# Small instructions of a top-k attention and mixture-of-depths kernel move from VectorE to GpSimd and ScalarE

## The chip, the cores and the metric

The kernel runs on one core of a Trainium2 chip. The metric is device time in microseconds of one execution; less is better. Five engines of the core work from queues of their own, each in the order of its program: TensorE (PE in profiles, PEld for its weight loads), VectorE (DVE), ScalarE (ACT), GpSimd (POOL) and SyncE (SP), which issues most of the DMAs.

## The reference

Two blocks follow each other. The first is attention over 8 batches, 8 heads, 576 tokens and a head size of 64, in which each query keeps its 32 highest scores:

```python
scores = scale * np.matmul(q, k.transpose(0, 1, 3, 2))
kth = np.partition(scores, -top_k, axis=-1)[..., -top_k:-top_k + 1]
scores = np.where(scores >= kth, scores, -1000000000.0)
attn = np.exp(scores - np.max(scores, axis=-1, keepdims=True))
attn = attn / (np.sum(attn, axis=-1, keepdims=True) + 1e-09)
x = np.matmul(attn, v)          # then (B, S, H*D) = (8, 576, 512)
```

The second is a mixture of depths: the 128 tokens of a batch with the highest gate score pass through a two-layer network, weighted by the sigmoid of their gate, and the other tokens stay:

```python
scores = np.einsum('bsd,d->bs', x, w_gate)
top_idx = np.argpartition(-scores[b], capacity)[:capacity]
ye = np.maximum(x[b, top_idx] @ w1, 0.0) @ w2
g = 1.0 / (1.0 + np.exp(-scores[b, top_idx]))
out[b, top_idx] = x[b, top_idx] + g[:, None] * ye
```

## The kernel before, in words

**Units and steps.** A batch's 576 tokens make five tiles: four of 128 tokens (`J` = 4) and one of 64. A unit is a tile and two heads (four heads in the short tile), so a batch has 18 units and the whole 144. The main loop is a software pipeline over the units. Step `n` does at once: the products of queries and keys of unit n+1 on TensorE and their copy to `sc` by ScalarE; `bound_of(n)` on VectorE, which finds a lower bound of the 32nd highest score by 14 MAX8 over parts of the row and a few more over the candidates; `sign(n-1)` on ScalarE, which compares each score with the bound (`sides`); `weigh_signs(n-1)` on GpSimd, which multiplies scores and signs to `y` and fills eight more columns; `kth_of(n-2)` on VectorE, two long MAX8 (`next`) that give the 32nd score; `mask_of(n-3)`, in which ScalarE marks what is below it for one head and GpSimd for the other (`less`); the transposes, exponentials (`pT`, `last`) and products with the values for unit n-4, and the copy of the values to `xs`.

**Order.** Every engine's instructions are kept in program order. Work that should stand late in a step is put on lists as a function and called at fixed places of the step: `late` (flushed on ScalarE between the mask and the copy of the scores), `vector_late` (between the two heads' first MAX8), `pool_late` (after that, ahead of `y`), `kept` (after the copy of the values) and `after_kth` (after `kth_of`, on VectorE). There is no planner; the steps at which the pieces of the second block run are written by hand in `mix_at` and `mix_at_of`.

**A finished tile.** In the step in which the last unit of a tile is done, `keep_sums` (line 710) has ScalarE copy the sums of the exponentials out of `xs` into `sums`. In the next step `normalise` runs from `vector_late`: a reciprocal `rden` on VectorE, then a product on GpSimd. A step later `gates` multiplies the tile with the gate weights (`prod`, `gate`). After the fifth tile the batch is stored, and `mixture` (line 761) starts, a generator whose pieces run in the following steps.

**The mixture.** It splits the gates into three bf16 parts (`split`), sends the gates through DRAM to have all 576 on every partition (`gate_row`), and then, tile by tile, counts on VectorE how many gates are higher (`choose`, line 800), which is the token's rank. A comparison of the rank with the numbers 0 to 127 gives a 0/1 matrix `pick`; for the first tile VectorE makes it in the same place, for the others GpSimd does (`choose_slot`). Five matmuls of `pick` with the parts put each slot's token number and gate, in three parts each, into PSUM. ScalarE copies them to `found`, and `add_up` (line 846) on VectorE adds the parts, forms the row number `row_i` and clips the gate; ScalarE takes the exponential, and `squash` adds one and inverts. GpSimd fetches the rows with an indirect DMA, TensorE multiplies, and GpSimd adds the result to the rows in DRAM with another.

**Masks beside scatters.** At the six `scatter_steps` the second half of the mask is not GpSimd's but VectorE's (`mask_of(n - 3, (act, None) ...)`, line 1207), through `vector_late`.

**Checks.** At the end VectorE reduces what was kept of the bounds (`bounded`, copied by ScalarE in `keep_least`), `least`, `seen` and `sums` to one number per partition, `sure`, and adds the sums of all `ranks` and of the last batch's `others`. TensorE adds over the partitions; if the total isn't the expected one, a general path computes everything again.

Of the kernel before, what the change touches and what calls it, by code (L numbers as in the profile page):

```python
# [19 lines left out]
CAP = 128  # L20
# [28 lines left out]
def kernel(  # L49
# [69 lines left out]
    for i in range(2):  # L119
        gate = const.tile([P, NT], FP32, name=f"gate{i}")  # L120
        nc.gpsimd.memset(gate, 0.0)
        parts = const.tile([P, NT, 2, 3], BF16, name=f"parts{i}")
        nc.gpsimd.memset(parts, 0.0)
        nc.vector.tensor_copy(out=parts[:, :, 0, 0:2], in_=parts_i)
        gates_of.append((gate, parts))
# [28 lines left out]
    ranks = const.tile([P, B, NT], FP32, name="ranks")  # L154
    nc.gpsimd.memset(ranks, 0.0)

    others = const.tile([P, NT], FP32, name="others")
# [51 lines left out]

    after_kth = []  # L210

# [373 lines left out]
    def mask(sc, next8, on=None):  # L585

        less = wkpool.tile([P, 2, S], BF16, name="less")  # L590
        for i, engine in enumerate(on or (act, pool)):
            kth = next8[:, i, 7:8]
            if engine is act:
                act.activation(less[:, i, :], sc[:, i, :], AF.Relu, bias=kth, scale=-1.0)
            else:

                def is_less(engine=engine, i=i, kth=kth):
                    if engine is None:
                        compare(less[:, i, :], sc[:, i, :], kth, ALU.is_lt)
                        return  # L600
                    engine.tensor_scalar(
                        out=less[:, i, :],
                        in0=sc[:, i, :],
                        scalar1=kth,
                        scalar2=None,
                        op0=ALU.is_lt,
                    )

                if engine:
                    is_less()  # L610
                else:
                    vector_late.insert(0, is_less)
        return less
# [95 lines left out]

    def keep_sums(n, xs, den):  # L710
        act.activation(den, xs[0:n, :, D], AF.Copy, bias=1e-9)

# [47 lines left out]

    def mixture(row0, pg, rank, exact=False):

# [31 lines left out]

        pick = modpool.tile([P, NT, CAP], BF16, name="pick")
        for t in range(NT):
            yield
            n = R if t == J else P

            def choose(t=t, n=n):  # L800
                junk = modpool.tile([P, S], FP32, name="junk", tag="scratch")
                dve.tensor_scalar(
                    out=junk[0:n, :],
                    in0=gate_row[0:n, :],
                    scalar1=gate[0:n, t : t + 1],
                    scalar2=None,
                    op0=ALU.is_gt,
                    op1=ALU.add,
                    accum_out=rank[0:n, t : t + 1],
                )  # L810
                if exact:
                    break_ties(t, gate, gate_row, rank)

                if t == 0:
                    compare(pick[:, t, :], slot, rank[:, t : t + 1], ALU.is_equal)
                else:
                    pool_late.append(lambda: choose_slot(t, n))

            def choose_slot(t, n):
                pool.tensor_scalar(  # L820
                    out=pick[0:n, t, :],
                    in0=slot[0:n, :],
                    scalar1=rank[0:n, t : t + 1],
                    scalar2=None,
                    op0=ALU.is_equal,
                )

            vector_late.append(choose)
# [4 lines left out]
        else:  # L833
            ps = values_bank[0]
        ps = ps[:, 2 * DE : 2 * DE + 6]

# [4 lines left out]
        multiply_places(ps, pick, pg)  # L841
        found = stats.tile([P, 6], FP32, name="found", bufs=2)
        place = stats.tile([P, 2], FP32, name="place", bufs=2)
        kept.append(lambda ps=ps: act.copy(out=found, in_=ps))

        def add_up():
            add_parts(place, found)
            keep_rows(
                place,
                row_i,  # L850
                row0 if isinstance(row0, float) else row0[:, 0:1],
                float(done * S - 1),
            )
            dve.tensor_scalar_max(out=g, in0=place[:, 1:2], scalar1=-88.0)
            late.append(lambda: act.activation(g, g, AF.Exp, scale=-1.0))

        def squash():
            dve.tensor_scalar_add(out=g, in0=g, scalar1=1.0)
            dve.reciprocal(out=g, in_=g)

        kept.append(lambda: after_kth.append(add_up))
        if exact:
            for todo in (kept, after_kth):
                while todo:
                    todo.pop(0)()
        yield
# [15 lines left out]
        for fc in range(NFC):  # L882
            yield
            if fc == 1:
                vector_late.append(squash)
            if fc % 2 == 0:
                ps = ps_misc.tile([P, 2, CAP], FP32, name="h_ps", tag="misc")
            multiply_h(ps[:, fc % 2, :], fc, xeT)
            if fc % 2 == 1:
                copies_late.append(  # L890
                    lambda ps=ps, fc=fc: act.activation(
                        hT[:, fc - 1 : fc + 1, :], ps, AF.Relu
                    )
                )
# [13 lines left out]
    def multiply_places(ps, pick, pg):  # L908

        for t in range(NT):  # L910
            n = R if t == J else P
            pe.matmul(
                ps,
                pick[0:n, t, :],
                pg[1][0:n, t, :, :].rearrange("p a e -> p (a e)"),
                start=(t == 0),
                stop=(t == J),
            )

    def split(gate, parts):  # L920

        rest = modpool.tile([P, NT], FP32, name="rest")
        pool.tensor_copy(out=parts[:, :, 1, 0], in_=gate)
        pool.tensor_tensor(rest, gate, parts[:, :, 1, 0], ALU.subtract)
        pool.tensor_copy(out=parts[:, :, 1, 1], in_=rest)
        pool.tensor_tensor(rest, rest, parts[:, :, 1, 1], ALU.subtract)
        pool.tensor_copy(out=parts[:, :, 1, 2], in_=rest)

    def add_parts(place, found):
        dve.tensor_reduce(  # L930
            out=place,
            in_=found.rearrange("p (a e) -> p a e", e=3),
            axis=mybir.AxisListType.X,
            op=ALU.add,
        )

    def keep_rows(ps, row_i, row0, most):

        dve.tensor_scalar(
            out=row_i,  # L940
# [184 lines left out]
    def keep_least(b, bound, kth):  # L1125
        at = 2 * per_batch * b
        late.append(
            lambda: act.copy(
                out=bounded[:, at : at + 2 * per_batch].rearrange("p (n i) -> p n i", i=2),
                in_=bound,  # L1130
            )
        )
        dve.tensor_reduce(
# [9 lines left out]
    for n in range(-1, N):  # L1143
# [62 lines left out]
        if is_unit(n - 3):  # L1206
            mask_of(n - 3, (act, None) if n in scatter_steps else None)
        flush()
# [22 lines left out]
        if is_unit(n - 4):  # L1231
# [13 lines left out]
            if g4 == groups(t4) - 1:  # L1245
                inverting = b4, t4, xs
                n4 = R if t4 == J else P
                keep_sums(n4, xs, sums[0:n4, b4 * NT + t4, :])
            while kept:
# [7 lines left out]
        if is_unit(n - 2):  # L1257
            kth_of(n - 2)
        while after_kth:
            after_kth.pop(0)()  # L1260


        if early:
            weigh_signs(n - 1)

        if gating is not None:
            b, t = gating
            if t == J:
                store(out[b], of_batch[b][0])
                mixtures[b] = mixture(float(b * S), of_batch[b][1], ranks[:, b, :])  # L1270
        for b in rest:
# [155 lines left out]
    for t in (J - 1, J):  # L1427
# [8 lines left out]
        )  # L1436
    ps = bank(ps_end, "av3")[:, 0:6]
    place = stats.tile([P, 2], FP32, name="place", bufs=2)
# [5 lines left out]
    xe = modpool.tile([P, HD], FP32, name="xe")  # L1444
    fetch_rows(xe, out, row_i)
    dve.tensor_scalar_max(out=g, in0=place[:, 1:2], scalar1=-88.0)
    act.activation(g, g, AF.Exp, scale=-1.0)
# [43 lines left out]
    for what, op, than, limit in (  # L1491
# [5 lines left out]
        (sums.rearrange("p t h -> p (t h)"), ALU.min, ALU.is_gt, FEWEST),  # L1497
        (sums.rearrange("p t h -> p (t h)"), ALU.max, ALU.is_lt, MOST),
    ):
        far = stats.tile([P, 1], FP32, name="far", bufs=2)  # L1500
# [4 lines left out]

    far = stats.tile([P, 1], FP32, name="far", bufs=2)
    dve.tensor_reduce(out=far, in_=ranks, axis=mybir.AxisListType.XY, op=ALU.add)
    dve.tensor_tensor(sure, sure, far, ALU.add)
    far = stats.tile([P, 1], FP32, name="far", bufs=2)
    dve.tensor_reduce(out=far, in_=others, axis=mybir.AxisListType.X, op=ALU.add)  # L1510
    dve.tensor_tensor(sure, sure, far, ALU.add)
    ones = stats.tile([P, 1], FP32, name="ones", bufs=1)
# [4 lines left out]
    for f0 in range(0, NFC, 2):  # L1517
# [22 lines left out]
        scalar1=-1.0,  # L1540
        scalar2=float(P + B * (S * (S - 1) // 2)),
        op0=ALU.mult,
# [135 lines left out]
```

## Time and profile before

| what | us |
|---|---|
| median of 3 executions (lowest, highest) | 802.77 (802.66, 803.39) |
| the profiled execution | 802.83 |
| its span, first to last instruction | 800.5 |
| VectorE busy | 771.6 |
| ScalarE busy | 728.4 |
| TensorE busy, matmuls | 728.1 |
| GpSimd busy | 706.4 |

A group of the page is one kind of instruction: its source line (nearly always 45 here, a helper that keeps the order), engine, operation, `out<-in`, shapes and count, then busy time and the mean length of one in ns. In a timeline a line begins with the start and the length in us; "x7" means that seven alike were merged. Neighbours on an engine overlap, so the distance from one start to the next can be shorter than the length.

### The profile page before, as it was taken

What the parts mean: (1) busy time and instruction counts of PE and PEld (TensorE: products, weight loads), DVE (VectorE), ACT (ScalarE), POOL (GpSimd) and SP (SyncE); (2) the same over time, 40 slices, a digit from 0 to 9 for tenths busy, and PEclk for the clock granted to TensorE, in tenths of its full rate; (3) what the DMA queues carried; (4) which work ended last, traced back from release to release, by engine and by line L of the source; (5) the groups of instructions that cost most, each with busy time, mean ns of one, the idle gap of its engine ahead of it and who ended that gap; (6) DMA issues with size and microseconds to landing.
All of it is one profiled execution on the core that took longest, in us unless ns stands there. A gap on an engine that the chain in (4) does not pass through costs nothing. (4 is left out here: it accounts for less than half of the span.)

```text
span 800.5 us, 33285 instructions
## 1 busy us (share of the span) xinstructions
PE 728.1 (91%) x12535; PEld 550.2 (69%) x12535; DVE 771.6 (96%) x4655; ACT 728.4 (91%) x1577; POOL 706.4 (88%) x722
## 2 busy tenths in 40 slices
PE   8888888788999999999999989999899999999887
PEld 6766666656876668766786667866687667767756
DVE  7999999999999999999999999999999999999962
ACT  6999999999999999999999999999999999989830
POOL 4899999899999999999999999999999999999921
PEclk9999999999999999999999999999999999999999
DMA  8941114121241132221251221502234102101021
GB/s 170 293 95 43 42 62 103 29 54 29 70 107 42 29 94 63 64 55 41 69 109 29 56 41 62 113 20 54 42 90 89 29 8 75 24 6 25 3 74 31
DMA packets 121752, 50.70 MB, mean 63 GB/s; under 512 B 116016, under 2 KB 116016, under 8 KB 120560
## 3 DMA queue, kind: packets, MB, share of 16 engines
q1 hardware_dynamic: 118368, 43.94, 22.2%
q0 software_dynamic: 1744, 4.20, 2.8%
q8 instruction: 101, 1.65, 0.9%
q10 hardware_dynamic: 1472, 0.36, 0.2%
q14 instruction: 67, 0.55, 0.2%
HBM read 36.93 MB, written 11.55 MB: 61 GB/s over the span
## 5 line engine op out<-in xcount | busy, mean ns | idle before, releaser
L45 POOL TENSOR_TENSOR y<-sc,sides 128x576 f32<-128x576 f32 x288 | 366.9, 1304 | 17.7 <-ACT sides L45 16.6
L45 DVE MAX8 cand<-sc 128x8 f32<-128x82 f32 (+1 forms) x2016 | 314.4, 228 | 3.0 <-ACT sc L45 3.0
L45 POOL TENSOR_SCALAR less<-sc,next 128x576 bf16<-128x576 f32 x135 | 232.5, 1722 | 38.4 <-DVE next L45 34.2
L45 ACT ACTIVATE sides<-sc,bound 128x576 bf16<-128x576 f32 x288 | 229.6, 797 | 17.0 <-DVE bound L45 13.1
L45 PEld LDWEIGHTS av<-v,pT 128*64 128x64 f32 x4608 | 146.9, 138 | 91.4 <-ACT last L45 83.8
L45 DVE MAX8 next<-y 128x8 f32<-128x584 f32 x288 | 204.4, 751 | 0.0
L45 PE MATMUL av<-v,pT 128*64 128x65 f32 x4608 | 166.9, 225 | 38.9 <-ACT last L45 38.4
L45 PEld LDWEIGHTS <-less 64*128 64x128 bf16 (+1 forms) x2448 | 157.6, 129 | 29.3 <-POOL less L45 24.6
L45 PE MATMUL ps<-kT,qT 64*128 64x288 f32 (+1 forms) x1248 | 170.1, 422 | 0.3 <-ACT sc L45 0.3
L45 PE MATMUL ptr<-out_of_reach,less 64*128 64x64 bf16 x2272 | 151.0, 190 | 17.3 <-POOL less L45 16.6
L45 PE MATMUL ptr<-ident,sc 64*128 64x64 f32 x2272 | 166.3, 252 | 0.0
L45 ACT ACTIVATE pT<-ptr 128x1024 f32<-128x1024 f32 x142 | 147.7, 1040 | 14.5 <-PE ptr L45 12.7
L45 ACT COPY sc<-ps 128x1152 f32<-128x1152 f32 x140 | 159.6, 1140 | 0.0
L45 PEld LDWEIGHTS ptr<-ident,sc 64*128 64x128 f32 x2272 | 138.6, 137 | 23.8 <-issue 21.2
L45 ACT ACTIVATE less<-sc,next 128x576 bf16<-128x576 f32 x141 | 110.5, 784 | 0.0
L45 PEld LDWEIGHTS ps<-kT,qT 64*128 64x128 f32 (+1 forms) x1248 | 92.8, 176 | 17.6 <-ACT sc L45 0.4
L45 DVE MATCH_REPLACE8 cand<-best,cand 128x21 f32<-128x21 f32 (+1 forms) x576 | 98.8, 179 | 0.0
L45 DVE MAX8 best<-cand 128x8 f32<-128x21 f32 (+1 forms) x576 | 90.4, 189 | 0.0
L45 ACT ACTIVATION_READ_ACCUMULATOR sides<-sc,bound 128x1 f32 x288 | 62.0, 215 | 0.0
L45 PE MATMUL h_ps<-xeT,w 128*128 128x128 f32 x464 | 61.9, 278 | 0.0
L45 PEld LDWEIGHTS av<-ident,sc 128*128 128x128 f32 x144 | 20.0, 139 | 54.8 <-issue 44.9
L45 PE MATMUL av<-vpair,last 128*64 128x130 f32 x576 | 56.9, 276 | 0.0
(165 smaller groups left out, 925.2 us busy)
## 6 DMA issues: line engine op xcount, KB each, us to landing
v<-in_v_dram SPq DMA_DIRECT2D x64, 128.0 KB, 3.7
out_dram<-x SPq DMA_DIRECT2D x8, 1024.0 KB, 4.1
rows<-in_k_dram SPq DMA_DIRECT2D x56, 128.0 KB, 2.8
rows<-in_q_dram SPq DMA_DIRECT2D x56, 128.0 KB, 2.9
w<-in_moe_w_dram SPq DMA_DIRECT2D x2, 2048.0 KB, 10.3
gate_row<-row_dram SPq DMA_DIRECT2D x7, 288.0 KB, 4.6
last<-in_q_dram SPq DMA_DIRECT2D x8, 128.0 KB, 3.6
vpair<-in_v_dram SPq DMA_DIRECT2D x16, 64.0 KB, 4.8
```

The source lines that it names most:

```text
L45: return lambda *a, **kw: self._tc.keep_in_program_order(fn(*a, **kw))
```

## The change

- The first tile's ranks (not on the general path) come from ScalarE: the sign of "own gate minus gate" over the 576 gates is summed with the accumulator; for rank r the sum is 575-2r. The signs themselves go into `pick` as scratch. GpSimd compares the sum with `slot_signs`, which holds 575-2s for slot s, and makes the first tile's `pick`.
- `choose` for the other tiles counts on VectorE as before; all `pick` are GpSimd's.
- The second half of the mask at scatter steps is made by ScalarE.
- `add_up`, with two additions in place of a reduction, and the plus one of `squash` (now `add_one`) run on GpSimd; `at_end`, which takes the place of `after_kth`, is flushed at the end of the step, after `weigh_signs`.
- `keep_sums` of the loop goes to `at_end` on GpSimd, and so does the copy to `bounded`, by `pool_late`, of all batches but the last.
- The parts have a seventh column of ones, so that the matmuls with `pick` also count how many tokens fill each slot (`places`). The end checks that this is one, and no longer sums `ranks` and `others`.

```diff
+    slot_signs = const.tile([P, CAP], FP32, name="slot_signs")
+    nc.vector.tensor_scalar(out=slot_signs, in0=slot,
+        scalar1=-2.0, scalar2=float(S - 1), op0=ALU.mult, op1=ALU.add)
...
-    def keep_sums(n, xs, den):
-        act.activation(den, xs[0:n, :, D], AF.Copy, bias=1e-9)
+    def keep_sums(n, xs, den, on=None):
+        if on is pool:
+            pool.tensor_scalar(
+                out=den, in0=xs[0:n, :, D], scalar1=1e-9, scalar2=None, op0=ALU.add
+            )
+        else:
+            act.activation(den, xs[0:n, :, D], AF.Copy, bias=1e-9)
...
+            def weigh_gates():
+                act.activation(
+                    pick.rearrange("p t c -> p (t c)")[:, 0:S],
+                    gate_row,
+                    AF.Sign,
+                    bias=gate[:, 0:1],
+                    scale=-1.0,
+                    accum_out=sign_sum,
+                )
+                pool_late.append(lambda: choose_slot(0, P, slot_signs, sign_sum))
+
+            if t == 0 and not exact:
+                late.append(weigh_gates)
+                continue
...
-                if t == 0:
-                    compare(pick[:, t, :], slot, rank[:, t : t + 1], ALU.is_equal)
-                else:
-                    pool_late.append(lambda: choose_slot(t, n))
+                pool_late.append(lambda: choose_slot(t, n))
...
         def add_up():
-            add_parts(place, found)
+            if exact:
+                add_parts(place, found)
+            else:
+                terms = found[:, 0:6].rearrange("p (a e) -> p e a", e=3)
+                pool.tensor_tensor(place, terms[:, 0, :], terms[:, 1, :], ALU.add)
+                pool.tensor_tensor(place, place, terms[:, 2, :], ALU.add)
             keep_rows(
                 place,
                 row_i,
                 row0 if isinstance(row0, float) else row0[:, 0:1],
                 float(done * S - 1),
+                dve if exact else pool,
             )
-            dve.tensor_scalar_max(out=g, in0=place[:, 1:2], scalar1=-88.0)
+            (dve if exact else pool).tensor_scalar_max(
+                out=g, in0=place[:, 1:2], scalar1=-88.0
+            )
             late.append(lambda: act.activation(g, g, AF.Exp, scale=-1.0))

+        def add_one():
+            (dve if exact else pool).tensor_scalar_add(out=g, in0=g, scalar1=1.0)
+
         def squash():
-            dve.tensor_scalar_add(out=g, in0=g, scalar1=1.0)
             dve.reciprocal(out=g, in_=g)

-        kept.append(lambda: after_kth.append(add_up))
+        kept.append(lambda: at_end.append(add_up))
...
+        if b < B - 1:
+            pool_late.append(lambda: pool.tensor_copy(out=to, in_=bound))
+        else:
+            act.copy(out=to, in_=bound)
...
-            mask_of(n - 3, (act, None) if n in scatter_steps else None)
+            mask_of(n - 3, (act, act) if n in scatter_steps else None)
...
-                keep_sums(n4, xs, sums[0:n4, b4 * NT + t4, :])
+                at_end.append(
+                    lambda a=(n4, xs, sums[0:n4, b4 * NT + t4, :]): keep_sums(*a, on=pool)
+                )
...
-        while after_kth:
-            after_kth.pop(0)()
-
-
         if early:
             weigh_signs(n - 1)
+        flush_end()
...
+        (places[:, :, 6], ALU.min, ALU.is_gt, 0.5),
+        (places[:, :, 6], ALU.max, ALU.is_lt, 1.5),
...
-    dve.tensor_reduce(out=far, in_=ranks, axis=mybir.AxisListType.XY, op=ALU.add)
-    dve.tensor_tensor(sure, sure, far, ALU.add)
-    far = stats.tile([P, 1], FP32, name="far", bufs=2)
-    dve.tensor_reduce(out=far, in_=others, axis=mybir.AxisListType.X, op=ALU.add)
-    dve.tensor_tensor(sure, sure, far, ALU.add)
...
```

## The prediction

> **What bounds the kernel now.** I read the page's busy shares first, then the slices, then VectorE's waits, then a table over equal periods, and last the timelines of single steps. The page's chain of waits is no help here: it holds only the last store (1.3 us).
>
> ```profile
> PE 728.1 (91%) x12535; PEld 550.2 (69%) x12535; DVE 771.6 (96%) x4655; ACT 728.4 (91%) x1577; POOL 706.4 (88%) x722
> DVE  7999999999999999999999999999999999999962
> DVE cand L45 <- ACT sc L45: 3.0, 3, 2.1
> DVE rden L45 <- ACT sums L45: 2.5, 2, 1.4
> ```
>
> VectorE is in the top tenth from the second slice to the 38th, and its list of waits has nothing inside the loop over steps: the 3.0 us for `cand` are in the first steps, the 2.5 us for `rden` in the tail. So it alone sets the pace of the loop. How near are the others? The next view gives span and busy us (PE, PEld, DVE, ACT, POOL) from the first tile's `rden` of a batch to that of the next, which is 18 steps:
>
> ```profile
> 45.16:135.62 90.46, 75.28 (x1478) 57.14 (x1476) 90.43 (x557) 89.57 (x195) 86.35 (x85) 1.00 0.28 66
> 418.85:513.41 94.56, 89.31 (x1551) 66.85 (x1550) 94.42 (x577) 90.91 (x198) 88.19 (x88) 1.00 0.25 60
> ```
>
> A steady period takes 94.56 us, with VectorE at 94.42, ScalarE 3.65 us short of it and GpSimd 6.4 us. What VectorE loses comes off the period until ScalarE's or GpSimd's own need is reached: that decides this case.
>
> **What the Trainium skill says.** "Perfetto Trace Analysis", § Optimizing Scalar/DVE Operations: when VectorE is saturated, moving work to ScalarE or GpSimd may pay, though GpSimd shares a port with VectorE. "SBUF — State Buffer", § Who interferes with whom: the `tensor_scalar` form that writes its accumulator, and reductions, do not contend for that port; so the removed instructions freed nothing on GpSimd, and I count no port effect. "Perfetto Trace Analysis", § GPSIMD Engine Instruction: time GpSimd by start-to-start spacing. The trace agrees that this matters: a cast of 128x5 is listed at 0.20 us, yet dependent ones follow at 0.28 and the one after the last starts after 0.15. "ScalarE: Activation LUTs", § What ACT_TABLE_LOAD costs: about 280 ns + 0.833 ns per element, neighbours overlapping by 93 ns. For 576 that is 760 ns; the trace has 784 to 797, and 0.67 us from start to start.
>
> **The change, part by part.** All durations below are start to start.
>
> *Off VectorE.* The first tile's rank and slots, an emptied mask, the sum of place parts, and `g` plus one:
>
> ```profile
> 418.85 0.18 DVE L45 RECIPROCAL rden<-sums 128x8 f32<-128x8 f32 x1
> 418.95 0.76 DVE L45 TENSOR_SCALAR_CACHE_REDUCE junk<-gate_row,gate 128x576 f32<-128x576 f32 x1
> ...
> 420.02 1.11 DVE L45 MAX8 cand<-sc 128x8 f32<-128x82 f32 x7
> 466.09 0.14 DVE L45 TENSOR_REDUCE place<-found 128x2 f32<-128x6 f32 x1
> ...
> 466.39 1.40 DVE L45 MAX8 cand<-sc 128x8 f32<-128x82 f32 x9
> 472.77 0.79 DVE L45 TENSOR_SCALAR_CACHE_REDUCE less<-sc,next 128x576 bf16<-128x576 f32 x1
> 473.49 0.08 DVE L45 DVE_READ_ACCUMULATOR less<-sc,next 128x1 f32 x1
> 488.04 0.13 DVE L45 TENSOR_SCALAR g<-g 128x1 f32<-128x1 f32 x1
> 488.21 0.16 DVE L45 RECIPROCAL g<-g 128x1 f32<-128x1 f32 x1
> ```
>
> Rank and slots 420.02-418.95 = 1.07; place, `row_i` and `g` 466.39-466.09 = 0.30; mask 473.49-472.77 = 0.72; `g` plus one 0.17. Seven batches have all but the mask, six have the mask (the other six such masks, in the tail, stay): 7 x (1.07+0.30+0.17) + 6 x 0.72 = 10.8 + 4.3 = 15.1 us. Summing durations instead would give 18.4, but neighbours overlap. A full period loses 2.26 and could be 92.3.
>
> *ScalarE.* Added per full period: the sum of signs, 0.77 (`sides` plus its accumulator read, 0.677+0.093), and the second mask, 0.67. Removed: five `sums` at 0.28 each (`xs` to `sums` to `pT` takes 0.31+0.12, without `sums` 0.15), and `bounded`, 0.15. Net 1.44-1.55 = -0.1: its need stays near 90.8. The seventh column of `found` costs nothing that 0.18 us would show.
>
> *GpSimd.* Added per full period: five `sums`, a `bounded`, one 128x128 pick, four instructions of add-up, one of `g` plus one. The trace has the pick at 0.57. For 128x8 or smaller it has no `tensor_scalar`; from below 0.15 (an independent cast), from above 0.27 (the straight line through picks, 0.57 for 128 elements, and masks, 1.69 for 576, carried to 8). I take 0.2: 5x0.2+0.2+0.57+(0.28+0.28+0.1+0.2)+0.2 = 2.8, between 2.4 and 3.5. Need 91.0, up to 91.7, under 92.3.
>
> *New waits.* (a) `rden` on VectorE now waits for `sums` on GpSimd, which stands behind the two products `y` and their fill of the step before. VectorE's next seven MAX8 and all later ones queue behind it. In the steady batches fill ends 1.2 to 1.5 us ahead of `rden` in tiles 1 to 4, and `sums` needs 0.2 to 0.3: hidden. In the first tile it ends 0.23 ahead (the split of the gates delays GpSimd): 0.1 lost. In batch 0 the fill is late, and GpSimd still runs behind ScalarE's first signs:
>
> ```profile
> 45.16 0.18 DVE L45 RECIPROCAL rden<-sums 128x8 f32<-128x8 f32 x1
> 45.89 0.22 POOL L45 TENSOR_TENSOR y<-steps,seen 128x16 f32<-128x16 f32 x1
> ```
>
> `sums` would end near 46.3, so VectorE stands 1.2 us, once. Sum of (a): 1.2 + 7 x 0.1 = 1.9.
> (b) The exponential of `g` on ScalarE now waits for GpSimd's add-up, and the score copy `sc` is queued behind it:
>
> ```profile
> 466.51 0.20 ACT L45 ACTIVATE g<-g 128x1 f32<-128x1 f32 x1
> 466.88 1.12 ACT L45 COPY sc<-ps 128x1152 f32<-128x1152 f32 x1
> 466.74 0.21 POOL L45 TENSOR_TENSOR y<-steps,seen 128x16 f32<-128x16 f32 x1
> 471.75 0.37 DVE L45 MAX8 cand<-sc 128x8 f32<-128x82 f32 x2
> ```
>
> GpSimd can start adding at 466.93 and needs 0.28+0.28+0.1+0.2, so `g` is there about 467.8: ScalarE stands 1.3 us. The copy ends at 468.00 and VectorE wants it at 471.75: 3.75 us of cover. The next step brings the mask (+0.67), VectorE comes 1.0 us earlier, 0.65 of ScalarE's idle time is used up, and the load copies up to the next batch eat cover in the kernel before too (2.2 left at its tightest, five steps on). Cover left: 2.2-1.2-0.7 = 0.3; then, at the sum of signs, 3.25-2.3-1.0 = 0. So VectorE is not stopped, or stopped by some tenths. In sum: ScalarE's need is 90.8+1.3 = 92.1 of 92.3. I charge 0.3 in each of the five periods that hold both, 1.5 us.
> (c) The sum of signs waits for the gate row, issued at 407.1 and landing 4.6 later, while it runs near 419; in batch 6 it has about 2 us. Nothing. Its sign output goes into `pick`, which the earlier batch's matmuls left a batch ago.
> (d) The row fetch on GpSimd issues some 0.8 us later, with three steps until TensorE wants it; batches 5 and 6 have two, but TensorE has slack there (1.0 us idle in that step). Nothing. GpSimd's next mask stands behind the add-up too, and through it `ptr` on TensorE and `pT` on ScalarE: about a microsecond later, in the shade of (b).
>
> *Start and end.* The one extra VectorE instruction and three memsets fit in 1.05 us that VectorE waits before its first copy. At the end two reductions with a combine (0.47 each) replace two of nearly the same size, under TensorE's matmuls; the one-column copy is hidden by the fetch of rows. Nothing.
>
> Sum on the profiled execution's 802.83: 802.83-15.1+1.9+1.5 = 791.1. It stands 0.06 us off the median of 802.77, so I forecast **791.1 us**.
>
> **Rivals.**
> *ScalarE or GpSimd becomes the bound.* For it: needs of 92.1 and 91.7 against 92.3, and each has stretches of several steps with no idle time. Against it: two to four microseconds of cover between engines. If GpSimd's small instructions cost 0.27 and the wait (b) is 1.8, a period cannot go under about 93.5: six periods gain 1.1 each, the last batch 1.5, less 1.2: 802.8-6.9 = 796, up to 799.
> *Slower: `rden` stalls.* 38 reciprocals now depend on GpSimd's queue. It decides from 15.1/38 = 0.40 us of mean stall, that is when `sums` ends 1.65 us after the fill where the cover is 1.25. One instruction that walks 8 elements at a stride of 65 would have to cost 1.5 us, or GpSimd to fall a microsecond behind for good. At 0.6 a tile: 802.8+22.8-15.1 = 810.5. Against: its waits for `next` (34.2 us) show that it gets ahead again in most steps.
> *The end check trips.* The sum of signs meets the slots' values only if the sign of zero is zero (a gate against itself). The skill's "ScalarE: Activation LUTs", § Step-by-step: what each stage is for, says only that zero gives a constant of the function; no row of the trace shows which. If it is another, the general path recomputes all eight batches, over a thousand us.
> *It does nothing:* would need a bound elsewhere at 94.5, which VectorE's list of waits excludes.
>
> **How the numbers follow.** My forecast 0.70 (788 to 795); another engine bounds 0.14 (795 to 800); slower by `rden` 0.10; check trips 0.02; within 0.2%, by stalls that happen to cancel, 0.04. A measurement of this kernel tells about 0.2% (1.6 us) from no change. Faster 0.84, same 0.04, slower 0.12. Low end: the whole 15.1 with nothing lost, 787.7, less a little; high end: the second case, 799.
>
> **What would show it.** Right: VectorE's busy time near 755 (the durations' 18.4 less), still in the top tenth; one wait of `rden` on `sums` near 1.2 at 45 us; a wait of ScalarE's `g` on GpSimd near 1.3, seven times; periods of 92.3 to 92.7. Wrong: `cand` waiting for `sc` by whole microseconds each period (second case), or `rden` waiting in most tiles (third).

## The result, and the profile after

The changed kernel takes 817.34 us (median of 4 executions, 816.17 to 817.80) where the kernel before takes 802.93 us (802.66 to 803.39) on the same chip: 1.0177 times as long, 95% interval 1.0159 to 1.0194. It is 14.4 us slower; the forecast was 11.7 us faster. The profiled execution took 817.8 us, its span 816.0 us, 15.5 us more than before.

The same views as before, of the changed kernel. First the page's busy times and VectorE's row of the slices:

```profile
PE 732.8 (90%) x12535; PEld 554.9 (68%) x12535; DVE 764.9 (94%) x4588; ACT 728.4 (89%) x1553; POOL 743.1 (91%) x812
DVE  7999999999999999999899998999899999999962
```

VectorE's slices now have eights inside the loop, where before there were only nines: it has begun to wait. Its busy time fell by 6.7 us only, not by the 15 to 18 of the forecast. GpSimd's rose by 36.7 us. VectorE's waits, and ScalarE's for `g`:

```profile
DVE rden L45 <- POOL sums L45: 22.0, 23, 2.0
DVE cand L45 <- ACT sc L45: 4.7, 5, 2.1
ACT g L45 <- POOL g L45: 12.1, 7, 1.9
```

The first line did not exist before: 23 of the 38 reciprocals stood, 22.0 us in all. A steady period, again from one batch's first `rden` to the next one's (columns as before: from:to, us, then busy us of PE, PEld, DVE, ACT, POOL):

```profile
428.74:525.44 96.70, 89.16 (x1552) 66.96 (x1551) 93.67 (x566) 90.96 (x195) 93.10 (x99) 1.00 0.25 61
```

It grew from 94.56 to 96.70 us, where 92.3 was forecast. GpSimd is now 93.10 us busy in it, against a forecast need of 91.0 to 91.7.

**One stall, close up.** The timeline of the changed kernel in the tile after an adding up; VectorE's lines, then GpSimd's; the bracket gives the idle time just before and who ended it:

```profile
490.79 1.11 DVE L45 MAX8 cand<-sc 128x8 f32<-128x82 f32 x7
493.71 0.20 DVE L45 RECIPROCAL rden<-sums 128x8 f32<-128x8 f32 x1 [1.81 <-POOL sums L45]
...
491.88 1.28 POOL L45 TENSOR_TENSOR y<-sc,sides 128x576 f32<-128x576 f32 x1 [0.58 <-ACT sides L45]
493.12 0.22 POOL L45 TENSOR_TENSOR y<-steps,seen 128x16 f32<-128x16 f32 x1
493.43 0.24 POOL L45 TENSOR_SCALAR sums<-xs 128x8 f32<-128x8 f32 x1
493.77 1.73 POOL L45 TENSOR_SCALAR less<-sc,next 128x576 bf16<-128x576 f32 x1
```

VectorE is done with the first head's seven MAX8 at 491.90 and wants to invert. The 0.24 us that it needs from GpSimd stand behind a product `y` and its fill, and it gets them at 493.67. From the start of the fill to the start of `less` GpSimd takes 0.65 us here; without `sums` between them it took 0.19 in the kernel before (a timeline below has both lines). So one `sums` takes some 0.45 us of GpSimd's queue, though its bar has 0.24.

**What does not show in a list of waits.** The row of VectorE's groups for `prod`, the product of a finished tile with the gate weights, which the change does not touch; before and after:

```profile
L45 DVE CUSTOM_DVE_ANT_0 prod<-x,wg 128x512 f32<-128x512 f32 (+1 forms) x40 | 30.5, 762 | 0.2
```

```profile
L45 DVE CUSTOM_DVE_ANT_0 prod<-x,wg 128x512 f32<-128x512 f32 (+1 forms) x40 | 36.4, 909 | 0.2
```

The same 40 instructions take 5.9 us more. GpSimd's fill of `y` did the same (here too before, then after):

```profile
L45 POOL TENSOR_TENSOR y<-steps,seen 128x16 f32<-128x16 f32 x144 | 34.7, 241 | 0.0
```

```profile
L45 POOL TENSOR_TENSOR y<-steps,seen 128x16 f32<-128x16 f32 x144 | 45.1, 313 | 0.0
```

These instructions keep their shape and get longer, so I take them to be waiting inside their own bars; the timelines below show for what. The sum for the profiled execution is then: 15.1 us removed; 5.9 us more in `prod`; VectorE's idle time 22.2 us more (28.9 to 51.1 us, span less busy). In each of the 23 stalls VectorE also loses the 0.08 us by which an unhindered `rden` begins before the end of the MAX8 ahead of it, 1.8 us in all. That makes +14.8 us of the 15.5 measured.

### The profile page after: what moved, and what is told of

It reads as the page before. It is cut to its first block, busy times and chain, and to the rows that moved or that the text cites. A ratio compares the mean times of both kernels' runs of the same rounds, so it can differ in the third digit from the quotient of the medians.

```text
span 816.0 us, 33292 instructions
## 1 busy us (share of the span) xinstructions
PE 732.8 (90%) x12535; PEld 554.9 (68%) x12535; DVE 764.9 (94%) x4588; ACT 728.4 (89%) x1553; POOL 743.1 (91%) x812
## 5 line engine op out<-in xcount | busy, mean ns | idle before, releaser
L45 POOL TENSOR_SCALAR less<-sc,next 128x576 bf16<-128x576 f32 x135 | 235.2, 1742 | 10.2 <-DVE next L45 6.3
L45 PEld LDWEIGHTS <-less 64*128 64x128 bf16 (+1 forms) x2448 | 159.6, 130 | 49.0 <-POOL less L45 46.5
L45 PE MATMUL av<-v,pT 128*64 128x65 f32 x4608 | 167.8, 225 | 27.7 <-ACT last L45 27.2
L45 PE MATMUL ps<-kT,qT 64*128 64x288 f32 (+1 forms) x1248 | 172.5, 426 | 0.6 <-ACT sc L45 0.6
L45 ACT ACTIVATE less<-sc,next 128x576 bf16<-128x576 f32 x147 | 114.9, 787 | 0.0
```

The costliest lines, as they stand in the source:

```text
L45: return lambda *a, **kw: self._tc.keep_in_program_order(fn(*a, **kw))
```

## The experiments

There are three theories. **One** is the place of the wait: VectorE stands because `rden` hangs behind the products `y` in GpSimd's queue. **Two** is the load: GpSimd simply has too much work, wherever it is waited for. **Three** was at first only a question about the longer `prod` and became a theory of its own after the first four runs: VectorE's `prod`, with two inputs in SBUF, and GpSimd's `y` exclude each other.

What each run measured ("ratio" is to the kernel before on the same chip, with its 95% interval; "waits" are those of `rden` for GpSimd's `sums`; `prod` is the group's total over 40). The kernel before took 802.8 to 803.7 us beside these runs:

| run | us, median | ratio | VectorE busy | waits | `prod` |
|---|---|---|---|---|---|
| before | 802.93 | 1 | 771.6 | 0 | 30.5 |
| after | 817.34 | 1.0177 (1.0159 to 1.0194) | 764.9 | 22.0 | 36.4 |
| after, sums on ScalarE | 806.75 | 1.0038 (1.0024 to 1.0053) | 774.1 | 0 | 47.1 |
| before, sums on GpSimd | 807.0 | 1.0053 (1.0033 to 1.0073) | 771.0 | 3.5 | 28.9 |
| after, sums between the products `y` | 813.81 | 1.0135 (1.0117 to 1.0153) | 778.1 | 4.6 | 49.7 |
| after, adding up on VectorE | 803.0 | 0.9995 (0.9984 to 1.0006) | 764.6 | 8.3 | 34.3 |
| before, `prod` 2.4 us later | 833.85 | 1.0383 (1.0362 to 1.0404) | 802.6 | 0 | 61.5 |
| after, sums on ScalarE, `prod` with one input | 787.9 | 0.9811 (0.9794 to 0.9827) | 754.5 | 0 | 26.7 |
| after, `prod` with one input | 800.0 | 0.9963 (0.9949 to 0.9977) | 755.1 | 15.5 | 26.7 |
| after, sums on ScalarE, adding up on VectorE | 796.05 | 0.9918 (0.9902 to 0.9935) | 764.0 | 0 | 35.5 |
| the same, `prod` 0.45 us later | 788.15 | 0.9811 (0.9785 to 0.9837) | 757.2 | 0 | 28.6 |
| before, `prod` 0.45 us later | 800.55 | 0.9965 (0.9952 to 0.9978) | 768.8 | 0 | 27.7 |
| before, adding up on GpSimd | 807.41 | 1.0041 (1.0021 to 1.0060) | 774.1 | 0 | 35.3 |
| after, `prod` 0.45 us later | 813.66 | 1.0126 (1.0104 to 1.0148) | 762.9 | 19.1 | 34.2 |

### The wait taken away: sums back on ScalarE

```diff
-                at_end.append(
-                    lambda a=(n4, xs, sums[0:n4, b4 * NT + t4, :]): keep_sums(*a, on=pool)
-                )
+                keep_sums(n4, xs, sums[0:n4, b4 * NT + t4, :])
```

> The changed kernel with the loop's sums back on ScalarE, directly after the copy of the values; all else of the change stays. Theory one (the place of the wait: VectorE stands because rden hangs behind the products y and the fill in GpSimd's queue): no rden wait in the loop, the 22 us come back, 792 to 797 us; prod then shows whether its stretch from 0.75 to 0.96 us belongs to the stalls (back to 0.8) or not (stays at 0.95). Theory two (GpSimd has too much work, wherever the wait stands): GpSimd sheds only 38 x 0.25 = 9.5 us of its 37 extra, so 808 to 812 us, and the waits of VectorE reappear at next<-y or at cand<-sc.

It took 806.75 us, which lies in neither range (1.3 us under theory two's), and it is still slower than the kernel before. The waits for GpSimd's `sums` are gone. They do not come back as waits for `y` or `sc`, where theory two looked for them (`cand` waits 4.0 us for `sc`, not more than the 4.7 in the changed kernel); `rden` waits 4.6 us for ScalarE's `sums`. Yet VectorE's busy time went up by 9.2 us. The groups of this kernel by shape, and then its timeline at one of the short tiles, VectorE's line first:

```profile
L45 DVE CUSTOM_DVE_ANT_0 prod<-x,wg 128x512 f32<-128x512 f32 x32 | 32.7, 1023 | 0.1
L45 DVE CUSTOM_DVE_ANT_0 prod<-x,wg 64x512 f32<-64x512 f32 x8 | 14.4, 1796 | 0.0
```

```profile
501.64 2.20 DVE L45 CUSTOM_DVE_ANT_0 prod<-x,wg 64x512 f32<-64x512 f32 x1
...
500.54 2.51 POOL L45 TENSOR_TENSOR y<-sc,sides 128x576 f32<-128x576 f32 x2
503.02 0.21 POOL L45 TENSOR_TENSOR y<-steps,seen 128x16 f32<-128x16 f32 x1
503.22 2.21 POOL L45 TENSOR_SCALAR less<-sc,next 128x576 bf16<-128x576 f32 x1
```

A `prod` that takes 0.67 us elsewhere takes 2.20 here. It ends at 503.84, 0.6 us after GpSimd's two products and their fill are through; and the `less` that follows on GpSimd takes 2.21 us instead of 1.72, so it seems to stand for the last part of `prod`: the two take turns. In the kernel before, the same `prod` of the same batch met `less`; its lines there, VectorE's first:

```profile
498.72 0.82 DVE L45 CUSTOM_DVE_ANT_0 prod<-x,wg 64x512 f32<-64x512 f32 x1
...
495.59 2.52 POOL L45 TENSOR_TENSOR y<-sc,sides 128x576 f32<-128x576 f32 x2
498.07 0.21 POOL L45 TENSOR_TENSOR y<-steps,seen 128x16 f32<-128x16 f32 x1
498.26 1.72 POOL L45 TENSOR_SCALAR less<-sc,next 128x576 bf16<-128x576 f32 x1
```

There `y` had ended 0.6 us before `prod` began; here it ended 1.4 us after. So at this `prod` the change, without its sums, has moved GpSimd two microseconds later against VectorE's step.

### One edit alone: only the sums on GpSimd

The same edit the other way round, put into the kernel before, flushed after `weigh_signs`.

> The kernel before, with only the loop's sums moved to GpSimd at the end of the step. Theory one (rden behind GpSimd's queue) in its strong form: the stalls come with this one edit, 22 us, 820 to 825 us. In its weak form: without the rest of the change GpSimd keeps its cover of 1.2 to 1.5 us in tiles 1 to 4, so only the first tile of batch 0 (1.2 us) and tenths in the other first tiles show: 804 to 807 us. Theory two (load): 9.5 us more on GpSimd of a slack of 45 us: no change, 802 to 804 us.

It took 807.0 us, the weak form's upper edge, and VectorE waited for `sums` five times, 3.5 us in all. The prediction had read 1.2 us for the first tile of batch 0 and 0.1 for the steady first tiles. The trace has 1.24, then 0.83 in the second and third batch, and 0.07 in the four after those; two more tiles of batch 0 have 0.3 each. So the reading of the cover was nearly right for this edit in that kernel. Beside the other edits the same dependence costs 22.0 us.

### The same load, another place: sums between the two products

```diff
         for i in range(2):
             pool.tensor_tensor(y[:, i, 0:S], sc[:, i, :], sides[:, i, :], ALU.mult)
+            while sums_late:
+                sums_late.pop(0)()
 ...
-                at_end.append(
+                sums_late.append(
```

> The changed kernel with the sums still on GpSimd, but issued between the two products y of the step, so that rden no longer stands behind the second product and the fill (some 1.5 us); GpSimd's load is the same. Theory one (place of the wait): rden waits fall under 5 us in all, 794 to 800 us. Theory two (load): GpSimd is as full as before this edit, 814 to 818 us.

The waits fell to 4.6 us as theory one expects, but the time did not: 813.81 us is 3.5 us less than the changed kernel takes, far from theory one's 794 to 800 us and just under theory two's 814 to 818. GpSimd stayed as full (747.1 us busy), and in a steady period it waits for another engine for 0.7 us only. The table says where the waits went: `prod` takes 49.7 us in all, 13.3 more than in the changed kernel. A VectorE that no longer stands for `rden` comes to `prod` while `y` still runs, and stands there. The place of the wait is therefore not the whole cause, and this run does not settle between one and two.

### The adding up back on VectorE

`add_up` uses `add_parts`, `keep_rows` and the clip on VectorE again, from the list after `kth_of`, and the plus one from `vector_late`; the sums stay on GpSimd.

> The changed kernel with the adding up of the place parts, the row number, the clip of g and the plus one back on VectorE; sums stay on GpSimd. GpSimd sheds 7 x (0.28+0.28+0.63+0.2+0.2) = 11 us, VectorE takes back 7 x 0.47 = 3.3 us. Theory one: the longest rden stall of a period (1.9 to 2.9 us, the tile after the add-up) goes, the first tiles' 0.8 stays: 817 - 7 x 2 + 3.3 = 806 us. Theory two (load): 817 - 11 + 3 = 809 us at the most gain, but rden's waits spread evenly rather than vanishing in that tile.

It took 803.0 us, below both: 14.3 us less for putting back 3.3 us of VectorE's work. The waits of `rden` fell from 22.0 to 8.3 us. In the changed kernel the fourth tile of the batches, which follows the adding up, waited 1.5 to 2.0 us; that is gone, and the 0.85 us in the first tiles stays, as theory one has it. GpSimd is 11.0 us less busy, which is also what theory two counts on; its most, 809 us, is passed by 6 us.

### Theory three: one instruction moved in the kernel before

```diff
-                if (i, u) == (1, 2) and amid_late:
-                    amid_late.pop()()
 ...
+        while amid_late:
+            amid_late.pop()()
```

> The kernel before with one instruction moved: prod (the product of a finished tile with the gate weights) stands after the candidates' MAX8, ahead of the two long MAX8 next, some 2.4 us later in its step. No instruction is added or taken away. There it meets GpSimd's products y, where before it met only less. Theory three (prod, with two inputs in SBUF, and GpSimd's two-input products y exclude each other, so that prod stands until y is through): prod grows from 0.76 us to 1.7 to 2.2 us on average, 40 x 1.2 = some 48 us at most, 820 to 850 us. Without such an effect: 802 to 804 us.

It took 833.85 us: 31 us more for moving one instruction, with none added. Its row:

```profile
L45 DVE CUSTOM_DVE_ANT_0 prod<-x,wg 128x512 f32<-128x512 f32 (+1 forms) x40 | 61.5, 1539 | 0.2
```

61.5 - 30.5 = 31.0 us in the group, 831.6 - 800.5 = 31.1 us in the span. The whole loss is in this one group, and it is there without anything of the change. It works in both directions, as the timeline of this kernel shows where `prod` came first (VectorE's line, then GpSimd's):

```profile
508.12 0.67 DVE L45 CUSTOM_DVE_ANT_0 prod<-x,wg 128x512 f32<-128x512 f32 x1
...
506.71 1.29 POOL L45 TENSOR_TENSOR y<-sc,sides 128x576 f32<-128x576 f32 x1
508.17 1.77 POOL L45 TENSOR_TENSOR y<-sc,sides 128x576 f32<-128x576 f32 x1 [0.17 <-ACT sides L45]
```

`prod` has its 0.67 us, and the `y` that was to start 0.05 us after it takes 1.77 in place of 1.29.

### Theory three against two: `prod` with one input

```diff
-        dve.tensor_tensor_reduce(
-            out=prod[0:n, 0:HD],
-            in0=x,
-            in1=wg[0:n, :],
 ...
+        compare(prod[0:n, 0:HD], x, 0.02, ALU.mult, g)
```

> The changed kernel with the sums back on ScalarE, as in the run with that edit alone (806.75 us), and with prod replaced by a product of x with one number, summed by the accumulator: one input in SBUF in place of two, of about the same length. This leaves the gate weights out of the computation. Theory three: no stretch, the instruction takes 0.7 us everywhere, 40 x (1.18 - 0.7) = 19 us come back, 786 to 790 us, which is about what the forecast was. Theory two (GpSimd's load, wherever it is waited for): VectorE then waits for y or for sc instead, 800 to 806 us.

> The changed kernel as it is, with prod replaced by the product of x with one number, summed by the accumulator: one input in SBUF. This leaves the gate weights out of the computation. Theory one (rden's waits) and theory three (prod against y) as separate costs that add up: 817.3 - 40 x (0.91 - 0.7) = 809 us, with the rden waits still near 22 us. If VectorE, being earlier, waits longer for rden instead: no change, 815 to 818 us.

With the sums on ScalarE it took 787.9 us, within theory three's range. The instruction now averages the undisturbed 0.67 us:

```profile
L45 DVE TENSOR_SCALAR_CACHE_REDUCE prod<-x 128x512 f32<-128x512 f32 (+1 forms) x40 | 26.7, 668 | 0.5 <-DVE junk L45 0.5
```

GpSimd is 718.5 us busy there, within 12.3 us of the 730.8 of the run with two inputs, and its order is the same. Theory two, which expected 800 to 806 us, falls for the kernel with the sums on ScalarE. Two limits of this run: the replacement is another kind of instruction as well as one with fewer inputs, so that the second input is what matters is not shown by it alone. And the kernel before has 3.8 us of its own to gain by the same replacement, if `prod` falls there too from 30.5 to 26.7 us (an estimate; it was not run).

In the changed kernel itself the same replacement gave 800.0 us, lower than either expectation. VectorE's waits, and two of GpSimd's groups:

```profile
DVE rden L45 <- POOL sums L45: 15.5, 20, 1.4
```

```profile
L45 POOL TENSOR_TENSOR y<-steps,seen 128x16 f32<-128x16 f32 x144 | 33.7, 234 | 0.0
L45 POOL TENSOR_SCALAR row_i<-place 128x1 int32<-128x1 f32 x7 | 1.7, 243 | 0.6
```

The `prod` itself gives 9.7 us. GpSimd, no longer held up by it, has its fill back at 234 ns (313 in the changed kernel) and `row_i` at 243 (630 there), so `sums` comes earlier and `rden` waits 6.5 us less: the conflict over `prod` had lengthened the other wait. Taken away from the changed kernel, GpSimd's sums are worth 10.6 us, the two-input `prod` 17.3, both together 29.4.

The 15.5 us that are left are not explained by `prod`. A steady period of this run, what GpSimd waits for in it, and then what it waited for in the same period of the kernel before (waits of 0.2 us or less left out):

```profile
418.83:513.20 94.37, 88.96 (x1552) 66.87 (x1551) 92.15 (x565) 90.88 (x195) 91.28 (x99) 1.00 0.25 61
```

```profile
POOL y L45 <- ACT sides L45: 0.6, 1, 0.6
POOL less L45 <- DVE next L45: 0.5, 1, 0.5
```

```profile
POOL less L45 <- DVE next L45: 5.5, 10, 1.0
```

Here VectorE stands 2.2 us of the period and GpSimd waits for another engine for 1.1 us. Its work with the spaces between its instructions so takes 93.3 us (94.37 less 1.1), where the kernel before had 88.9 (94.56 less 5.5 and 0.2): 4.4 us more, and more than the 92.3 us that VectorE would need. With the sums on GpSimd, then, load and place go together, and no run separates theory one from theory two for the 12.1 us between 800.0 and 787.9; the sums between the two products together with a one-input `prod` were not tried.

### Both parts put back, and then `prod` moved

The first of these is the changed kernel with the sums on ScalarE and the adding up on VectorE; the second moves `prod` as well:

```diff
-                if (i, u) == (1, 2) and amid_late:
+                if (i, u) == (1, 5) and amid_late:
```

> The changed kernel with both the sums back on ScalarE and the adding up (place parts, row number, clip, plus one) back on VectorE. What stays of the change: the first tile's sum of signs, its pick on GpSimd, the mask on ScalarE, bounded on GpSimd, the end check. VectorE is relieved of 7 x 1.07 + 6 x 0.72 = 11.8 us. Theory one and three together: GpSimd keeps its cover, no rden waits, prod mostly meets less as before (mean 0.75 to 0.85 us): 791 to 796 us. If the sum of signs and the mask on ScalarE alone upset the order: above 800 us.

> The kernel with sums back on ScalarE and the adding up back on VectorE (796.05 us), and prod three MAX8 later in its step (before the second head's sixth instead of its third, 0.45 us). In the trace of that kernel prod there begins 0.3 to 0.5 us after less in most steps and ends 1.28 us after less began, so 0.1 to 0.35 us too late; three MAX8 later it falls where less no longer holds it up. Theory three: mean of prod from 0.89 to 0.72 to 0.78 us, 796 - 5 = 791 us, 789 to 793. If the wait is not GpSimd's reads: no change, 795 to 797 us.

> The kernel before with the same move of prod alone, three MAX8 later (0.45 us). Before has prod at 0.82 us in two tiles of five and 0.67 in the others, so at most 40 x (0.76 - 0.68) = 3 us: theory three expects 799 to 802 us. It is the control for the gain of the other run: what the move is worth without the change.

They took 796.05 us and 788.15 us; the second is the fastest of those that keep the gate weights, 0.9811 of the kernel before (0.9785 to 0.9837). A steady period of it:

```profile
414.32:506.67 92.35, 88.74 (x1552) 66.85 (x1550) 92.28 (x571) 91.27 (x201) 89.52 (x90) 1.00 0.26 63
```

The period is about the forecast's 92.3 us, reached with less moved off VectorE and with `prod` at 28.6 us in all, below the 30.5 of the kernel before. VectorE is busy in all but 0.07 us of it. The move alone, in the kernel before, is worth 0.35% (800.55 us); so what is left of the change is worth 800.55 - 788.15 = 12.4 us, where 7 x 1.07 + 6 x 0.72 = 11.8 us had been taken from VectorE.

### Two controls

> The kernel before, with only the adding up (place parts, row number, clip, plus one) moved to GpSimd at the end of the step. VectorE is relieved of 7 x 0.47 = 3.3 us; GpSimd gets 1.5 us more in one step per batch and ScalarE waits for g. Inside the whole change the same edit costs 10.7 us (806.75 against 796.05 us). If it costs that by itself, because prod then meets y in the steps that follow: 808 to 814 us. If GpSimd, which has more idle time here, catches up before the next prod: 799 to 803 us.

> The changed kernel as it is, with prod three MAX8 later (0.45 us), the move that was worth 7.9 us after the two parts had been put back (796.05 to 788.15 us). Here rden still stands behind GpSimd's queue and GpSimd is later by more than 0.45 us. Theory one and three: prod gains 2 to 6 us of its 9.7 us stretch at most, and the rden waits (22 us) stay: 811 to 817 us. If the position of prod is all that was wrong: under 805 us.

The adding up alone on GpSimd costs 3.7 us against the 803.7 us of the kernel before beside it, which lies between the two cases named. Its `prod` takes 35.3 us, 4.8 more, and VectorE waits 2.5 us longer for `sc` and for ScalarE's `sums`; together that outweighs the 3.3 us saved. In the changed kernel the 0.45 us later `prod` gave some 4 us only, with 19.1 us of `rden` waits left, as expected: a shift that helps where GpSimd keeps its place in the step does not help where it comes later.

## Why the prediction was wrong

The measured time is 26.2 us above the 791.1 of the forecast. Two steps failed, with about half of that each, some 13.5 and 12.7 us by the estimate below.

**"I count no port effect": this step failed.** The prediction asked of the removed instructions only whether they share a port with GpSimd, and found that they do not. The question was to be asked of those that stay, since the change moves GpSimd's products in time against them. The skill's "SBUF — State Buffer", § Who interferes with whom, has the rule that was needed: a VectorE instruction with two inputs in SBUF contends with a GpSimd instruction that reads SBUF, by an exclusive lock, and the order of issue decides which of the two stands. `prod` is the only long instruction of that kind in the loop, and the trace agrees: beside two products `y` and their fill it took 2.20 us in place of 0.67. The profile before already held the sign of it, 762 ns on average, but 0.67 in some tiles and 0.82 in others. That the wait lies at `prod` is shown by the run that moved it alone (31 us) and by those that replaced it; that it is the second input rests on the page. It cost 17.3 us in the changed kernel (800.0 against 817.34), by itself and through the waits that it lengthens. Of these the kernel before has some 3.8 us too (30.5 - 26.7), so the change added about 13.5; both are estimates. Without the conflict the change would still have been only about level with the kernel before.

**GpSimd's price and the cover of wait (a): this step failed too.** The small instructions were taken at 0.2 us from start to start, between 0.15 and 0.27. Their bars fit that (0.244 for `sums`, 0.243 for `row_i` where nothing blocks it), but by start to start, as the prediction meant it, a `sums` takes some 0.45 us and the four of the adding up 1.08 where 0.86 was taken (both with the one-input `prod`). In place of 2.8 us per period, at most 3.5, the change gave GpSimd 4.4: 5 x 0.45 for `sums`, 0.31 for `bounded`, 0.58 for the pick, 1.08 for the adding up and 0.19 for the plus one. That is also the difference found above between the two kernels' periods. So its need was not 91.0 to 91.7 but 92.6 by the same sum, no longer under VectorE's 92.3. The cover of 1.2 to 1.5 us in tiles 1 to 4 was read in the kernel before, and held there (3.5 us in the run with that edit alone). With the adding up, the pick and the rest on GpSimd as well it did not: 1.9 us of waits for `rden` were charged, 15.5 measured with the one-input `prod`, and 22.0, 0.58 us a tile, with the conflict on top (10.4 us more in the fills, 2.7 in `row_i`). The 34.2 us of waits for `next`, from which the prediction concluded that GpSimd "gets ahead again in most steps", were the reserve that the change used up; 6.3 us of them are left. With the one-input `prod`, the sums back on ScalarE bring 12.1 us back. Whether the place of `sums` in the queue or GpSimd's whole load decides stays open.

Two rivals had each a part of it: GpSimd as the bound, put at 796 to 799 us, where the run without the conflict took 800.0 (some 804 with the 3.8 us that the kernel before has of it too), and the stalls of `rden`, whose 810.5 us at 0.6 a tile left out the longer `prod`. Part of those stalls came from the conflict, which no rival named.

**The bound: right where GpSimd stays out of the way.** With the sums and the adding up put back and `prod` moved, VectorE was relieved of 11.8 us and 12.4 came back, as shown above. It is not right for every kernel here: in the changed kernel with the one-input `prod` VectorE stands 2.2 us of a period and GpSimd has only 1.1 us to spare. That the run of 787.9 us came out at the forecast's low end, 787.7, is luck: some 3.8 us of its gain belong to the replaced `prod`.

**Wait (b): named, but too small.** ScalarE's `g` was to wait 1.3 us seven times. It waited 1.94 to 1.95 in six batches and 0.42 in the last (12.1 us in all), and 1.5 at the most with the one-input `prod`. VectorE's waits for `sc` rose by 1.7 us where 1.5 was charged, but there VectorE is late for other reasons. In the run of 787.9 us, where it isn't, they rose by 3.2 us (3.0 to 6.2), 0.64 in each of five periods in place of 0.3.

**Start, end, the check: right.** VectorE's first MAX8 begins at 7.68 us instead of 7.63. The time stays near 800 us, so the general path, for which the prediction reckoned with over a thousand more, did not run.

## What to carry to other kernels

Before work goes from VectorE to GpSimd, list the VectorE instructions that stay and read two operands from SBUF, and see in the timeline what GpSimd does at that moment. A later GpSimd can lengthen them without any wait showing in a list, so compare mean lengths of unchanged groups first. Price a small GpSimd instruction by how much later its successor starts, not by its bar (0.45 against 0.24 us here). A cover read in the kernel before holds for one edit; for several, subtract what each of the others spends of it before it is called hidden. And a stall that is removed can only come out as time if what VectorE then reaches earlier is not blocked too.

## What was not expected of the hardware

- How long GpSimd keeps `prod` out differs by its instruction. Beside `y` (two inputs, 1.28 us) `prod` stood to about its end. Beside `less` (one input, 1.72 us) it stood only at first: in the kernel before it ended 1.28 us after `less` began when it had started 0.46 us into it, and took its plain 0.67 us when it started a microsecond in. This is narrower than the lock for the whole instruction, of which the same page speaks in § SBUF: two separate sides, and the measurement decides. That `less` holds the port only while it reads would explain it; that is not shown.
- Between two products `y` that follow without a gap, a waiting `prod` was let in at some times and not at others: in the changed kernel with its sums on ScalarE, 0.90 us at some tiles of 128 tokens, and 2.20 us, past both products and the fill, at the short ones.
- VectorE's long MAX8 `next`, with one input, kept its mean of 751 ns in the changed kernel as in the one before, though GpSimd was 36.7 us busier.
